# DeltaNet recurrence and low-rank mixer on one core: the engine order written by the program's own planner

## Chip, core and metric

One core of one Trainium2 chip. The metric is the device time of one execution, in microseconds. The engines are TensorE (PE; its weight loads are listed as PEld), VectorE (DVE), ScalarE (ACT), GpSimd (POOL) and SyncE (SP, which here only issues DMAs). Each runs its own instructions in order, and waits for the others through semaphores.

## What is computed

Four batches of eight heads, 768 positions, head size 48, go through a delta-rule recurrence. The result, seen as `x` of 4 x 768 x 384, goes through a mixer. q, k, v and beta are float32; U, V and the two channel weights arrive as float64.

```python
k_n = k / (norm(k, axis=-1) + 1e-6)
for t in range(768):                       # state: 48 x 48 per batch and head
    y[:, :, t] = q_t @ state
    state = state + beta_t * outer(k_t, v_t - k_t @ state)
x = y as (4, 768, 384)                     # heads side by side
u = x + transpose(transpose(x) @ U @ V)    # U: 768 x 32, V: 32 x 768
out = u + relu(u @ w_ch1) @ w_ch2          # w_ch1: 384 x 1536, w_ch2: 1536 x 384
```

## The kernel before

**Units.** A batch `b` is cut into 12 chunks of 64 positions. Six chunks are a unit, `n = 2b` and `n = 2b + 1`. Inside a chunk the recurrence becomes a triangular system, whose inverse is found per unit for all its chunks and heads at once; the chunks themselves then follow one another through the state. Each unit goes through these steps:

- `load(n)` (lines 199 to 212): 24 DMAs on SP, eight each for k, q and v. `kn` and `vn` have two buffers, `qn` has one.
- `norms(n)` (214 to 250): square, sum, root and reciprocal of the keys' length, and `vn` times the length on GpSimd (line 237); one small transpose and four DMAs give `cp`, the factors that the inversion needs.
- `grams(n)` (252 to 295): 24 transposes of k and q (line 264) and 96 products of k with k and q (line 276), copied to `pg` and `qk`.
- `blocks(n)` (297 to 350): `pg` goes through DRAM (four DMAs `scr`, line 303, one DMA `gs`, line 310) to 96 partitions of 32 x 32 blocks. 31 steps of two VectorE instructions (lines 324 and 330) invert them in `xt`. Another trip through DRAM (lines 336 to 349: one DMA out, six back) puts the result into `zt` and `zc`.
- `below(n)` (352 to 390): two rounds of 96 small matmuls (`p_x`, line 364, and `p_v`, line 379) fill the off-diagonal block of `zt`.
- `recur(b, c)` (398 to 488), per chunk: matmuls `p_b`, a subtraction on VectorE to `rhs`, `p_y`, then `p_c`, a copy on ScalarE to `z`, then `p_s`, an addition on VectorE to the state, and the second part of `p_y`, copied into `x`. Each chunk needs the state of the one before.

**Mixer.** `mixer(b)` (491 to 546) needs all 12 chunks of its batch. `p_tt` is the product with U (line 495). Then, for each half of 384 positions: three times `p_h` (product with V, line 507), its addition to `x`, and three transposes `p_u`, copied to `ut`; then 12 times `p_f` (line 521; three matmuls of 384 columns and a relu on ScalarE), and three times `p_o` (line 535; 12 matmuls, an addition, and the output DMA of line 545). A float32 matmul stands in the trace as two records, so the 72 program matmuls of `p_f` and `p_o` of one half are 144 records, and all eight halves are 1,152.

**Weights.** `load_weights` (148 to 194) turns 27 slices of float64 into float32, 15 of them w_ch1, V and U, 12 w_ch2. Each slice is one DMA on SP into `wide` (two buffers), seven integer and float instructions on VectorE and a last addition on GpSimd (line 192).

**Order.** Every step is a Python generator. A heap (lines 549 to 582) holds for each generator a due time that is written by hand, and emits the steps by due time: `FIRST, PERIOD = 95.0, 140.0`, one batch per period. The emitted order is what the framework's own scheduler starts from; it may still reorder instructions.

Of the kernel before, what the change touches and what calls it, by code (L numbers as in the profile page):

```python
# [25 lines left out]
def kernel(  # L26
# [64 lines left out]

    ident = const.tile([128, 128], FP32, name="ident")
# [20 lines left out]

    betas = const.tile([128, NC, 4 * B], FP32, name="betas")
# [5 lines left out]
    def load_beta():  # L120
        beta_sb = unit.tile([4 * B, NC, 2, L], FP32, name="beta_sb", tag="kq")
        for b in range(B):
            for g in range(2):
                nc.sync.dma_start(
                    out=beta_sb[4 * b : 4 * b + 4, :, g],
                    in_=beta[b, 4 * g : 4 * g + 4, :].rearrange("s (c t) -> s c t", t=L),
                )
        p_bt = ps_one([128, NC, 4 * B], "p_bt")
        for c in range(NC):
            nc.tensor.transpose(  # L130
                p_bt[:, c], beta_sb[:, c].rearrange("r g t -> r (g t)"), ident[0 : 4 * B, 0 : 4 * B]
            )
        nc.vector.tensor_copy(out=betas, in_=p_bt)

    WIDE = 384

    def weight_slices():
        for t in range(KT):
# [3 lines left out]
        for s0 in range(0, S, WIDE):  # L142
            yield v_sb[:, s0 : s0 + WIDE], moe_V[:, s0 : s0 + WIDE], None
        yield u_sb.rearrange("p c r -> p (c r)"), moe_U, NB
# [3 lines left out]
    def load_weights():  # L148
# [3 lines left out]

        for dst, src, groups in weight_slices():
# [4 lines left out]
            if groups:  # L158
                to = to.rearrange("p (c r) -> p c r", c=groups)
                src = src.rearrange("(c p) r -> p c r", c=groups)  # L160
            nc.sync.dma_start(out=to, in_=src)
            yield
# [5 lines left out]
                out=power, in0=h, scalar1=0x7FF00000, scalar2=None, op0=ALU.bitwise_and  # L168
            )
            nc.vector.tensor_scalar(  # L170
                out=power, in0=power, scalar1=float(896 << 20), scalar2=float(1151 << 20),
                op0=ALU.max, op1=ALU.min,
            )
            nc.vector.tensor_scalar(
                out=power, in0=power, scalar1=float(896 << 20), scalar2=8.0,
                op0=ALU.subtract, op1=ALU.mult,
            )
            nc.vector.scalar_tensor_tensor(
# [3 lines left out]
            nc.vector.tensor_scalar(  # L182
                out=upper, in0=h, scalar1=3, scalar2=0x007FFFFF,
                op0=ALU.logical_shift_left, op1=ALU.bitwise_and,
            )
            nc.vector.tensor_tensor(out=upper, in0=upper, in1=power, op=ALU.bitwise_or)
            rest = power.bitcast(FP32)
            nc.vector.scalar_tensor_tensor(  # L188
                out=rest, in0=low, scalar=2.0 ** -52, in1=rest,
                op0=ALU.mult, op1=ALU.mult,  # L190
            )
            nc.gpsimd.tensor_tensor(  # L192
                out=dst, in0=upper.bitcast(FP32), in1=rest, op=ALU.add
            )
# [4 lines left out]
    def load(n):  # L199

        b, hf = divmod(n, 2)
        vn = unit.tile([128, UC, 4, D], FP32, name="vn")
        for t, src in ((kns[n % 2], k), (qn, q), (vn, v)):
            for g in range(2):
                for s in range(4):
                    nc.sync.dma_start(
# [5 lines left out]
        raw[n] = vn  # L212

    def norms(n):

        b, hf = divmod(n, 2)
        kn, vn = kns[n % 2][:, :, :, 0:D], raw[n]
        ksq = single.tile([128, UC, 4, D], FP32, name="ksq", tag="gs")
# [5 lines left out]
        yield  # L224
# [12 lines left out]
        nc.gpsimd.tensor_tensor(  # L237
            out=vn, in0=vn, in1=norm[:, :, :, None].to_broadcast([128, UC, 4, D]), op=ALU.mult
        )
        yield  # L240
# [9 lines left out]
        made[n, "c"] = cp  # L250

    def grams(n):

        kn = kns[n % 2]
        kq = unit.tile([128, UC, 2, 2, 2 * L], FP32, name="kq")
# [41 lines left out]
    def blocks(n):  # L297
# [23 lines left out]
        for j in range(BK - 1):  # L321
# [11 lines left out]
            if j % 4 == 3:  # L333
                yield
# [278 lines left out]
```

## Time and profile before

| | us |
|---|---|
| median of three runs | 915.73 (910.38 to 916.62) |
| the profiled execution | 915.65 |
| its span, from the first to the last instruction | 913.9 |
| TensorE busy | 706.4 (77%) |
| VectorE busy | 362.9 (40%) |
| ScalarE busy | 178.6 (20%) |
| GpSimd busy | 59.3 (6%) |
[...]
| share of the 16 DMA engines taken by SP's queue | 20.8% |

TensorE has 7,484 matmul records, 1,152 of them the wide ones of the mixer. The page sums busy time over the span; matmuls overlap, so the sums of single lines are larger than their share of the engine. All DMAs of the program stand on one queue, SP's, 43.08 MB in 150,672 packets, most of them under 512 bytes.

### The profile page before, as it was taken

Reading aid. Unit: us, or ns where it says so; the run is one execution under the profiler, and the core shown is the slowest. Engines: PE = TensorE matmul, PEld = TensorE weight load, DVE = VectorE, ACT = ScalarE, POOL = GpSimd, SP = SyncE. Lnnn points to the kernel's source line nnn. Section 1 sums busy time; section 2 is a strip of 40 time slices with the busy share of each in tenths; the row PEclk is TensorE's granted clock in tenths of the full one; section 3 lists DMA queues with packets and bytes.
Section 4 is the critical chain, followed back from the end, with each engine's and each line's share of the span. In section 5 each row is a group of like instructions: output and inputs, shape, how many; then the busy total and the mean of one; then the engine's idle time right before and its main releaser. Section 6 shows DMA issues by size and latency. Waiting matters only on the chain.

```text
span 913.9 us, 17342 instructions
## 1 busy us (share of the span) xinstructions
PE 706.4 (77%) x7484; PEld 437.0 (48%) x7484; DVE 362.9 (40%) x930; ACT 178.6 (20%) x386; POOL 59.3 (6%) x66
## 2 busy tenths in 40 slices
PE   2305604778988998704899899947999999999898
PEld 1204503564554565504465465625655565455454
DVE  1595798455944611282237113561363110100000
ACT  2103100231222212301331034102420231020020
POOL 2102112110210000100000001000100000000000
PEclk9756555576998999855599799975899799989799
DMA  3534314343231201402230212122102000000000
GB/s 77 119 89 111 80 44 122 71 96 88 69 68 46 44 19 37 81 8 48 50 62 19 51 30 55 42 60 54 28 10 69 2 3 10 17 1 9 17 0 27
DMA packets 150748, 44.19 MB, mean 48 GB/s; under 512 B 142928, under 2 KB 146000, under 8 KB 150672
## 3 DMA queue, kind: packets, MB, share of 16 engines
q1 hardware_dynamic: 150672, 43.08, 20.8%
q8 instruction: 59, 0.97, 0.4%
q14 instruction: 17, 0.14, 0.0%
HBM read 31.95 MB, written 11.01 MB: 47 GB/s over the span
## 4 chain that ended last, share of the span: by engine, by line
PE 64%; DVE 22%; ACT 4%; DMA 3%; SPq 3%; issue 3%; POOL 1%; ACTq 0%; DVEq 0%
PE p_f L521 21%; PE p_o L535 18%; DVE xt L330 6%; DVE prod L324 5%; PE p_c L441 3%; PE p_h L507 3%; PE p_y L473 3%; PE p_t L264 2%; PE p_g L276 2%; PE p_s L455 2%; PE p_tt L495 2%; PE p_u L514 2%; PE p_y L429 2%; PE p_v L379 2%; PE p_x L364 2%
## 5 line engine op out<-in xcount | busy, mean ns | idle before, releaser
L521 PE MATMUL p_f<-ut,w_sb 128*128 128x384 f32 x576 | 223.2, 533 | 3.4 <-ACT ut L515 3.4
L535 PE MATMUL p_o<-w_sb,h_f 128*128 128x384 f32 x576 | 196.2, 494 | 1.8 <-POOL w_sb L192 1.8
L521 PEld LDWEIGHTS p_f<-ut,w_sb 128*128 128x128 f32 x576 | 111.6, 205 | 74.6 <-issue 14.9
L535 PEld LDWEIGHTS p_o<-w_sb,h_f 128*128 128x128 f32 x576 | 107.9, 191 | 72.9 <-POOL w_sb L192 2.0
L330 DVE TENSOR_TENSOR xt<-xt,prod 96x31 f32<-96x31 f32 (+15 forms) x248 | 89.5, 361 | 7.0
L324 DVE TENSOR_TENSOR prod<-gs,xt 96x31 f32<-96x31 f32 (+15 forms) x248 | 84.9, 342 | 7.3
L544 DVE TENSOR_TENSOR x<-x,p_o 128x384 f32<-128x384 f32 x24 | 13.3, 553 | 179.5 <-PE p_o L535 179.5
L529 ACT ACTIVATE h_f<-p_f 128x384 f32<-128x384 f32 x96 | 47.1, 490 | 134.2 <-PE p_f L521 133.8
L364 PE MATMUL p_x<-zt,pg 32*32 32x32 f32 x768 | 19.4, 211 | 44.4 <-DMA zt<-scr 44.4
L425 DVE TENSOR_TENSOR rhs<-vn,p_b 128x192 f32<-128x192 f32 x44 | 15.5, 353 | 92.5 <-PE p_b L417 92.5
L495 PE MATMUL p_tt<-x,u_sb 128*32 128x384 f32 x48 | 23.3, 610 | 31.6 <-POOL u_sb L192 28.6
L464 DVE TENSOR_TENSOR s<-s,p_s 128x192 f32<-128x192 f32 x40 | 14.1, 354 | 82.7 <-PE p_s L455 82.7
L364 PEld LDWEIGHTS p_x<-zt,pg 32*32 32x32 f32 x768 | 17.5, 126 | 53.2 <-issue 49.2
L264 PE MATMUL p_t<-ident,kn 128*128 128x128 f32 x96 | 30.8, 342 | 15.7 <-DMA kn<-in_k_dram 15.7
L482 ACT COPY x<-p_y 64x192 f32<-64x192 f32 x96 | 30.0, 313 | 52.1 <-PE p_y L473 51.5
L276 PE MATMUL p_g<-kq 48*64 48x128 f32 x768 | 35.6, 319 | 5.4 <-ACT kq L269 4.0
L441 PE MATMUL p_c<-rhs,zt 64*64 64x48 f32 x704 | 34.3, 246 | 6.8 <-DVE rhs L425 6.8
L515 ACT COPY ut<-p_u 128x384 f32<-128x384 f32 x24 | 11.5, 478 | 141.8 <-PE p_u L514 141.8
L441 PEld LDWEIGHTS p_c<-rhs,zt 64*64 64x64 f32 x704 | 29.5, 160 | 19.6 <-DVE rhs L425 18.0
L473 PE MATMUL p_y<-z,qk 64*64 64x48 f32 x768 | 36.6, 242 | 1.9 <-ACT z L449 1.9
L372 ACT COPY xz<-p_x 64x768 f32<-64x768 f32 x8 | 6.3, 792 | 150.3 <-PE p_x L364 150.3
L192 POOL TENSOR_TENSOR w_sb<-upper,power 128x384 f32<-128x384 f32 x24 | 24.7, 1028 | 158.9 <-DVE power L188 158.9
(69 smaller groups left out, 647.3 us busy)
## 6 DMA issues: line engine op xcount, KB each, us to landing
wide<-in_moe_w_ch_dram SPq DMA_DIRECT2D x24, 384.0 KB
kn<-in_k_dram SPq DMA_DIRECT2D x64, 72.0 KB
qn<-in_q_dram SPq DMA_DIRECT2D x64, 72.0 KB
vn<-in_v_dram SPq DMA_DIRECT2D x64, 72.0 KB
out_dram<-x SPq DMA_DIRECT2D x24, 192.0 KB
scr<-pg SPq DMA_DIRECT2D x32, 96.0 KB
gs<-scr SPq DMA_DIRECT2D x8, 384.0 KB
scr<-xt SPq DMA_DIRECT2D x8, 384.0 KB
```

The source lines that it names most:

```text
L264: nc.tensor.transpose(p_t[:, j, i], t[:, c, 2 * j : 2 * j + 2].rearrange("p s d -> p (s d)"), ident,)
L276: nc.tensor.matmul(p_g[cols, par, c, :, j], kq[rows, c0 + c, j, 0, cols], kq[rows, c0 + c, j, :, cols], start=True, stop=True,)
L324: nc.vector.tensor_tensor(out=prod, in0=gs[:, j : j + 1, j + 1 :].to_broadcast([NP, m, w]), in1=xt[:, 0:m, j : j + 1].to_broadcast([NP, m, ...
L330: nc.vector.tensor_tensor(out=xt[:, 0:m, j + 1 :], in0=xt[:, 0:m, j + 1 :], in1=prod, op=ALU.subtract)
L364: nc.tensor.matmul(p_x[BK * g : BK * g + BK, r, BK * (e % (2 * UC)) : BK * (e % (2 * UC)) + BK], pg[rows, r, c, j, 0:BK], zt[rows, r, c, j ...
L441: nc.tensor.matmul(p_c[half(g), 2 * j + par], zt[half(g), par, cu, j], rhs[half(g), 2 * j + par], start=True, stop=True,)
L473: nc.tensor.matmul(p_y[half(g), par, D * j : D * j + D], qk[half(g), par, cu, j], z[half(g), 2 * j + par], start=(c == 0 and j == 0), stop ...
L482: nc.scalar.copy(xs[b][half(c % 2), c // 2, 4 * D * g : 4 * D * (g + 1)].rearrange("p (j r d) -> p r j d", r=2, d=D), pair_of(p_y)[half(g)],)
L495: nc.tensor.matmul(p_t, u_sb[:, c], x[:, c], start=(c == 0), stop=(c == NB - 1))
L521: nc.tensor.matmul(p_f, w1_sb[:, t, f * 128 : (f + 1) * 128], ut[:, t], start=(t == 0), stop=(t == KT - 1),)
L529: nc.scalar.activation(h_f, p_f, ACTF.Relu)
L535: nc.tensor.matmul(p_o, hs[f][:, c * 128 - g : (c + 1) * 128 - g], w2_sb[:, f], start=(f == 0), stop=(f == FT - 1),)
```

## The change

The heap of due times goes. Each step now yields, ahead of its instructions, either keys to wait for or three estimates: its TensorE time, its VectorE time, and a delay until its follower is ready. `run` keeps one clock for TensorE and one for VectorE and always emits the part whose step can start first by these estimates; between equals the part that stands earlier in the list wins. The list has the fronts of the mixer first, then batch by batch the recurrence, loads, norms, grams and blocks, with the weights behind those of batch 0, and at the end the wide parts of the mixer. All of it is traced in `tc.manual_schedule()`: each engine's order is then the emitted one.

Estimates that matter below: a load is ready 8.0 us after it is emitted, `gs` 6.0 us after the grams, `zt` 6.0 us after the inversion. A load's 24 issues take no time in the estimate, nor does a weight slice's DMA.

Besides the order: (1) beta comes in two DMAs instead of eight, on ACT's queue, and half of the k and q loads of unit 0 go there too; (2) the weight slices are loaded from GpSimd's queue, and U and V come first; (3) a slice takes five VectorE instructions and one on ScalarE, none on GpSimd; (4) `vn` is scaled on VectorE; (5) the mixer is split into `front(b, i)` and `wide(b, i)`, and the front takes its PSUM from the buffers `one`, not `mix`; (6) unit 1 has buffers of its own for the inversion (those of `ut`), and may start its trip through DRAM while unit 0 is inverted; (7) `below` is a part of `blocks`; `recur` runs through a whole batch.

```diff
+    def run(parts):
+        waits = {}
+        ready = {}
...
+        while waits:
+            best = None
+            for i in sorted(waits):
+                step = waits[i]
+                while i in waits and isinstance(waits[i][0], tuple):
+                    keys = [k for k in waits[i] if k[1] >= 0]
+                    if not all(k in done for k in keys):
+                        break
+                    advance(i, max([ready[i]] + [done[k] for k in keys]))
...
+                pe, dve, _ = waits[i]
+                start = max(ready[i], clock["pe"] if pe else 0, clock["dve"] if dve and not pe else 0)
+                if best is None or start < best[0] - 1e-6:
+                    best = start, i
...
+            if pe:
+                clock["pe"] = end
+            if dve:
+                end = clock["dve"] = max(end, clock["dve"]) + dve
+            clock["now"] = end
+            advance(i, end + after)
...
-            nc.sync.dma_start(out=to, in_=src)
-            yield
+            nc.gpsimd.dma_start(out=to, in_=src)
+            return dst, wide
...
+            yield 0, 1.3, 0.8
...
             nc.vector.tensor_scalar(
-                out=power, in0=h, scalar1=0x7FF00000, scalar2=None, op0=ALU.bitwise_and
+                out=power, in0=h, scalar1=20, scalar2=0x7FF,
+                op0=ALU.logical_shift_right, op1=ALU.bitwise_and,
+            )
+            nc.scalar.activation(
+                power, power, ACTF.Relu, bias=bias_e[0:rows], scale=2.0 ** 23
             )
...
     def load(n):
         b, hf = divmod(n, 2)
+        yield ("grams", n - 1), ("rec", n - 2)
+        yield 0, 0, 0
...
+                    queue = nc.scalar if n == 0 and g == 1 and t is not vn else nc.sync
+                    queue.dma_start(
...
+        emitted(("load", n), 8.0)
...
-        nc.gpsimd.tensor_tensor(
+        nc.vector.tensor_tensor(
             out=vn, in0=vn, in1=norm[:, :, :, None].to_broadcast([128, UC, 4, D]), op=ALU.mult
         )
...
     def blocks(n):
+        pool, tag = (mix, "ut") if n == 1 else (single, None)
+        yield ("grams", n), ("inverted", n - 1 - (n == 1))
+        yield 0, 0, 6.0
...
+            yield 0, 2 * (m * w + 150) / 960, 0.0
...
+        emitted(("inverted", n), 0.0)
+        yield ("below", n - 1),
+        yield 0, 0, 6.0
...
+    def recur(b):
+        yield ("mixed", b - 2), ("rec", 2 * b - 1)
...
+            yield (1.1, 0.4, 0.2) if c > 0 else (0, 0, 0)
...
+            yield 0.6, 0, 0.9
...
+            yield 1.1, 0.4, 0.2
...
+    def front(b, i):
+        yield (
+            ("rec", 2 * b + 1), ("front", b - (i == 0), 1 - i), ("wide", b - 1, i), ("weights", FT + 1)
+        )
...
+    def wide(b, i):
+        yield ("front", b, i), ("narrow", b - (i == 0), 1 - i)
+        for f in range(FT):
+            yield 1.95, 0, 0
...
+    parts = [beta_thread()]
     for b in range(B):
+        parts += [front(b, 0), front(b, 1)]
+    for b in range(B):
+        parts.append(recur(b))
+        for n in (2 * b, 2 * b + 1):
+            parts += [load(n), norms(n), grams(n)]
+        parts += [blocks(2 * b), blocks(2 * b + 1)]
+        if b == 0:
+            parts.append(load_weights())
+    for b in range(B):
+        parts += [wide(b, 0), wide(b, 1)]
+    with tc.manual_schedule():
+        run(parts)
```

## Rows read from the trace of the kernel before

**Rows 1.** The page, part 2: TensorE's busy tenths in 40 slices.

```profile
PE   2305604778988998704899899947999999999898
```

**Rows 2.** Stretches: us; PE, PEld, DVE, ACT, POOL busy; clock, DMA share, GB/s.

```profile
40.00:60.00 20.00, 2.24 (x19) 1.22 (x19) 18.49 (x53) 0.58 (x1) 0.00 (x0) 0.50 0.39 91
...
0.00:217.80 217.80, 96.75 (x1699) 72.59 (x1699) 133.35 (x345) 40.24 (x83) 37.49 (x46) 0.62 0.40 92
...
217.80:913.90 696.10, 609.67 (x5786) 364.46 (x5786) 229.53 (x585) 138.40 (x303) 21.78 (x20) 0.88 0.15 35
...
700.00:720.00 20.00, 17.48 (x77) 8.69 (x77) 3.09 (x5) 1.93 (x4) 0.00 (x0) 0.74 0.19 41
```

**Rows 3.** SP's queue, first 40 us: start us, us of issuing, line, count.

```profile
6.43 5.38 SPq L206 DMA_DIRECT2D kn<-in_k_dram  x8
...
25.88 0.51 SPq L161 DMA_DIRECT2D wide<-in_moe_w_ch_dram  x1
...
30.10 2.14 SPq L303 DMA_DIRECT2D scr<-pg  x4
...
32.29 1.27 SPq L206 DMA_DIRECT2D kn<-in_k_dram  x2
```

**Rows 4.** Timeline of VectorE and TensorE, first 226 us: start us, us, line.

```profile
30.78 0.35 DVE L167 TENSOR_SCALAR power<-wide 128x384 int32<-128x384 int32 x1
...
37.51 1.22 DVE L312 TENSOR_TENSOR gs<-gs,cp 96x1024 f32<-96x1024 f32 x1 [3.67 <-DMA gs<-scr]
...
91.38 1.08 PE L441 MATMUL p_c<-vn,zt 64*64 64x48 f32 x14 [0.36 <-ACT zt L385]
...
203.69 1.09 PE L473 MATMUL p_y<-z,qk 64*64 64x48 f32 x16 [0.47 <-ACT z L449]
...
217.78 7.78 PE L521 MATMUL p_f<-ut,w_sb 128*128 128x384 f32 x18 [0.57 <-ACT ut L515]
```

**Rows 5.** Chain of waits that ended last: start us, us, what.

```profile
11.18 2.38 DMA kn<-in_k_dram
...
80.80 2.95 DMA zt<-scr
...
389.80 1.23 DVE gs L312
...
414.26 2.99 DMA scr<-xt
...
422.20 2.78 PE p_x L364 x94
...
887.15 23.23 PE p_o L535 x72
```

**Rows 6.** Timeline of TensorE at the full clock, later stretches.

```profile
377.99 1.16 PE L276 MATMUL p_g<-kq 48*64 48x128 f32 x32 [0.24 <-ACT kq L269]
...
719.36 1.79 PE L364 MATMUL p_x<-zt,pg 32*32 32x32 f32 x94
...
740.80 0.45 PE L455 MATMUL p_s<-z,kn 64*64 64x48 f32 x16
...
745.37 0.45 PE L455 MATMUL p_s<-z,kn 64*64 64x48 f32 x16
...
790.25 4.06 PE L495 MATMUL p_tt<-x,u_sb 128*32 128x384 f32 x12
...
803.45 1.01 PE L521 MATMUL p_f<-ut,w_sb 128*128 128x384 f32 x1 [0.57 <-ACT ut L515]
```

**Rows 7.** Groups by line and shape: count, busy us, mean ns, idle before.

```profile
L167 DVE TENSOR_SCALAR power<-wide 128x384 int32<-128x384 int32 x24 | 8.4, 350 | 5.4 <-POOL w_sb L192 4.7 <-POOL u_sb L192 0.7
...
L178 DVE SCALAR_TENSOR_TENSOR power<-wide,power 128x384 int32<-128x384 int32 x24 | 13.2, 551 | 0.3
...
L192 POOL TENSOR_TENSOR w_sb<-upper,power 128x384 f32<-128x384 f32 x24 | 24.7, 1028 | 158.9 <-DVE power L188 158.9
```

**Rows 8.** Line 227 alone: ns minimum, median, maximum; first, last start.

```profile
L227 DVE TENSOR_TENSOR rec<-rec x8: 171/977/1922, 18.3 to 645.1; 128x24 f32<-128x24 f32 x8
```

More of the change, by code (lines that the diff above doesn't have):

```diff
@@ L89, in ps_mix, with emitted, advance @@
         return psum.tile(shape, FP32, name=name, tag="mix", bufs=2)
+    done, clock = {}, {"now": 0.0, "pe": 0.0, "dve": 0.0}
+    def emitted(key, after=0.0):
+        done[key] = clock["now"] + after
+    def run(parts):
+        waits = {}
+        ready = {}
+        def advance(i, at):
+            try:
+                waits[i], ready[i] = next(parts[i]), at
+            except StopIteration:
+                waits.pop(i, None)
+        for i in range(len(parts)):
+            advance(i, 0.0)
+        while waits:
[7 more added lines that the diff above has]
+                    advance(i, max([ready[i]] + [done[k] for k in keys]))
+                if i not in waits or isinstance(waits[i][0], tuple):
+                    continue
+                pe, dve, _ = waits[i]
+                start = max(ready[i], clock["pe"] if pe else 0, clock["dve"] if dve and not pe else 0)
+                if best is None or start < best[0] - 1e-6:
+                    best = start, i
+            start, i = best
+            pe, dve, after = waits[i]
+            end = start + pe
+            if pe:
[4 more added lines that the diff above has]
+            advance(i, end + after)
     ident = const.tile([128, 128], FP32, name="ident")
@@ L160, in load_weights @@
                 src = src.rearrange("(c p) r -> p c r", c=groups)
-            nc.sync.dma_start(out=to, in_=src)
-            yield
+            nc.gpsimd.dma_start(out=to, in_=src)
+            return dst, wide
+        slices = list(weight_slices())
+        yield 0, 0, 0
+        loaded = [start(*slices[0])]
+        for i in range(len(slices)):
+            dst, wide = loaded.pop()
+            rows, n = dst.shape
+            if i + 1 < len(slices):
+                loaded.append(start(*slices[i + 1]))
+            yield 0, 1.3, 0.8
             h, low = wide[0:rows, :, 1], wide[0:rows, :, 0].bitcast(U32)
@@ L181, in load_weights @@
             )
[L182 to L187, printed above, removed]
             nc.vector.scalar_tensor_tensor(
-                out=rest, in0=low, scalar=2.0 ** -52, in1=rest,
+                out=dst, in0=mant, scalar=2.0 ** -20, in1=power.bitcast(FP32),
                 op0=ALU.mult, op1=ALU.mult,
             )
-            nc.gpsimd.tensor_tensor(
-                out=dst, in0=upper.bitcast(FP32), in1=rest, op=ALU.add
-            )
+            emitted(("weights", len(slices) - i))
     raw, made, xs, states = {}, {}, {}, {}
@@ L236, in norms @@
         )
[L237 to L240, printed above, removed]
+        yield 0.3, 1.3, 0.5
         p_ct = ps_one([CS, 128], "p_ct")
@@ L389, in below @@
             )
-        yield
+        emitted(("below", n), 2.0)
     def by_slot(t):
@@ L549 @@
-    heap = []
-    def at(time, dt, fn, *args):
-        heap.append((time, len(heap), dt, fn, args, None))
-    MIX_STEPS = 1 + (S // GT) * (4 * (GT // 128) + FT + 2 * (GT // 128))
-    FIRST, PERIOD = 95.0, 140.0
-    load_beta()
-    for n in range(2 * B):
-        b, hf = divmod(n, 2)
-        t0 = (-40.0, -18.0, 27.0, 50.0)[n] if n < 4 else FIRST + PERIOD * (b - 2) + 65.0 * (hf + 1)
-        at(t0, 0, load, n)
-        at(t0 + 3, 1, norms, n)
-        at(t0 + 4, 1, grams, n)
-        at(t0 + 14, 2.5, blocks, n)
-        at(t0 + 38, 1, below, n)
```

372 lines of the change are left out of this document (192 added, 180 removed).

## Prediction

> **What bounds the kernel now.** I read the slices of the page first, then the busy time by stretch, then the timeline of the start, and last the chain of waits. In the slices [rows 1] TensorE is at 0 to 6 tenths in the first seven and falls to 0 and 4 again in slices 18 and 19 and to 4 in slice 27; the reader is to see two stages, and holes in the second. The first wide matmul of the mixer, `p_f`, starts at 217.78 us [rows 4]. Until there TensorE is busy for 97 of 218 us at a mean clock of 0.62, VectorE for 133 [rows 2]. Then come 696.1 us with TensorE busy for 609.7 at a clock of 0.88. So stage one is a chain of latencies that runs through VectorE and DMAs; stage two is bound by TensorE, with 86 us of idle time and a clock that is not always the full one.
>
> **How much of stage two is work.** I price TensorE's work after 217.78 at the full clock [rows 6]:
> - wide matmuls: 23.23 us for 72 records [rows 5], 0.3226 each; 1,152 make 371.7.
> - a chunk of the recurrence: two `p_s` are 4.57 us apart with three pairs of wide records between them, 4.57 - 6 x 0.3226 = 2.63; 36 chunks of batches 1 to 3 make 95.
> - grams: three times 1.16 for `p_g`; a transpose of 128 columns at a third of `p_tt`'s 4.06 / 12 is 0.11, 24 of them 2.7; together 6.2, and five units (3 to 7; unit 2 is done by then) make 31.
> - `below`: `p_x` 1.79, `p_v` alike, 3.5; six units make 21.
> - fronts: 4.06 for `p_tt`, and six times 0.68 + 3 x 0.11, 10.1 per batch; less the first half of batch 0, which lies before, 34.
>
> Together 553 of 696. The lost 143 are 86 idle and some 57 of low clock (among the idle is the tail from the last `p_o`, 887.15 + 23.23, to the span's 913.9: 3.5).
>
> **Stage one, part by part.** *Start.* Beta's eight issues stand ahead of k's at 6.43 [rows 3]; they go to ACT's queue, with half of unit 0's k and q. An issue on SP takes 5.38 / 8 = 0.67 us, and the last lands 2.38 later [rows 3, 5]. Unit 0's keys could land at about 9.5 instead of 13.6. But the planner counts no DMA time for weights and puts two to three slices of conversion ahead of `norms(0)` on VectorE; I let POOL's queue begin at 6, an assumption, as it clears the program's buffers first, and the first slice land at 10. So I give back half: `grams(0)` ends at 27 instead of 30. On ACT's queue ten issues, 6.7 us, stand ahead of the first square, which needs the keys anyway.
>
> *SP's order, against the change.* Before, the heap's times put `blocks(0)` ahead of `load(1)`, yet `kn` issues stand between `scr` and `gs` [rows 3]: the framework filled SP's waits. Now the order is the program's, and `load(1)`, which waits for the same key and stands earlier in the list, is emitted ahead of `blocks(0)`: 24 x 0.67 = 16 us. SP, with `cp(0)` at 20 to 23 by estimate, issues the load until 39. From the first `scr` (30.10) to the product on `gs` (37.51) it is 7.4 us [rows 3, 4], so inversion 0 begins at 47 instead of 37.5.
>
> *Inversions.* Alone, one takes 414.26 - 389.80 - 1.23 = 23.2 us [rows 5]. Inversion 0 with its product and unit 1's norms and masks (6.7 by the planner's estimates, taken as 6) ends at 77. The way back through DRAM is 422.20 - 414.26 = 8.0 us [rows 5], and 7.6 lie between the last `zt` (83.75) and `p_c` (91.38) [rows 4, 5]: recurrence 0 begins at 93, where it began at 91. Then the gain: inversion 1 follows at once, since unit 1 has buffers of its own and the weights come after both in the list. Before, batch 0's twelve chunks took from 91.4 to 204.8 [rows 4], 113 us where twelve at 4.6 are 55; the rest was inversion 1, with weight slices between its steps. It ends now at 77 + 24.4 + 5 (the chunks' own VectorE steps, 12 x 0.4) = 107, recurrence 1 can begin at 123, and recurrence 0 (six chunks at 4.6, the spacing of rows 6) ends at 121. So batch 0 is through at 123 + 28 = 151 instead of 204.8 [rows 4].
>
> *Weights.* A slice takes 2 x 0.35 + 3 x 0.551 = 2.35 us of VectorE, not 3.05 [rows 7]; ScalarE's new instruction lies on an engine busy for 40 of 218 us [rows 2]. Some seven slices fit before inversion 0 and eight more between 107 and 151, the 15 that the front asks for. This is cover, not gain, as long as the slices land. A load on POOL's queue is not in this trace. On SP the first slice was issued at 25.88 and used at 30.78 [rows 3, 4], so at most 4.9 us; from above I bound it in rival C. I take 5: two in flight then cost (5 + 2.35) / 2 = 3.7 us a slice, a little over the planner's 3.4, so VectorE waits a few us in all. On POOL the clearing of `xt` (lines 316 and 317) is queued behind a slice's issue, which waits for a conversion two slices back; VectorE has that conversion ahead of the inversion too, so it costs nothing more. `vn` on VectorE costs about 1.4 us (1,152 against `gs`'s 1,024 elements in 1.22 us [rows 4]) times eight, and frees VectorE of GpSimd: the 24-element product of line 227 takes 0.17 at least and up to 1.92 [rows 8], I take it while GpSimd's product of line 237 runs. I put these at nothing together.
>
> *Front.* From the end of the recurrence to `p_f` it was 13.0 us [rows 4]; I add 4, since now all six pairs of `p_tt` (4.06 [rows 6]) come after it. `p_f` starts at 151 + 17 = 168.
>
> **Stage two.** The wide parts stand last in the list, so they fill whatever the others leave, and the fronts get other PSUM buffers and run under the previous batch's `p_o`. That removes two kinds of loss: TensorE waiting for an inversion (slices 18, 19 and 27 [rows 1]; one inversion stands from 389.80 to 422.20 [rows 5]), and fronts standing alone (790.25 to 803.45, 13.2 us for 7.1 of work [rows 6]). New waits come from estimates that are too short, because TensorE now has to stand at the place the planner chose:
> - load: 8.0 (plus 1.0 for the recurrence's end) against 16 issues at 0.67 and 2.38, 13.1. Four us for each of units 2 to 7, 24. Behind the waiting transposes stand the wide matmuls, and all follow.
> - the way back to `zt`: 6.0 against 8.0, six times 2, 12.
> - `gs`: 6.0 against 7.4, on VectorE, where `rhs` and `s` of the running recurrence are queued behind it, six times 1.4, 8.
>
> Together 44. A wait costs clock as well: the stretch from 700 has 2.5 us of idle time in a front and a clock of 0.74, that is 5.2 us lost to the low level [rows 2]. I add 28 for the six loads and six `zt`. S = 72, half of what is lost now. Its bounds: 20 (waits fall together, the clock holds) and 143 (nothing is won).
>
> **Sum.** 168 + 553 + 72 + 3.5 for the tail = 796.5, and 1.75 that the execution lies over its span: 798. The profiled execution (915.65) is at the median of the runs (915.73), so the sum can be set against that.
>
> **Rivals.**
> A. The waits hide: S near 20, and the start as computed: 168 + 553 + 20 + 5 = 746. For it: a late load and a late `zt` may fall in one stall; recurrence, inversion and wide work are independent. Against: 20 us with a clock of 0.74 from 2.5 us of idle.
> B. TensorE stands as much as before: S = 143, 168 + 553 + 143 + 5 = 869. SP's in-order queue is what would do it, a 16 us load ahead of an inversion's `zt`; it is emitted first whenever a recurrence ends just before an inversion.
> C. Slower: slices on POOL's queue starve. GpSimd's addition took 1.03 us [rows 7]; if issuing a slice took as long, and only VectorE's idle time counted (1.51 of 20 us from 40 to 60 [rows 2]), a slice would come every 13.6 us. All 27 gate `p_o`: 6 + 27 x 13.6 = 373 instead of 168 + 23 = 191; some 50 us of recurrence and grams can be done meanwhile, so 798 + 182 - 50 = 930. It decides from about 13 us a slice. For it: rows 8. Against: what was waited out there is at most 1.75 us, and a conversion's instructions are 0.35 to 0.55 long [rows 7].
> D. The order comes out no better than the framework's: waits move from inversions to loads in both stages, about 915.
>
> [...]
>
> **Chances and range.** The forecast's case (750 to 845) 0.58, A 0.20, B 0.13, C 0.05, D 0.04. A measurement of this kernel can tell about 1% from no change. Faster by over 1% is the forecast, A and B: 0.91; within 1% D: 0.04; slower C: 0.05. The range goes down to `p_f` at 150 with S = 20 (728, rounded to 725) and up to `p_f` at 190 with S = 130 (878, rounded to 880); C, D and the ends of A and B stay out, under 2 in 10.
>
> **What would show it.** Right: `p_f` first at about 168; TensorE busy in nearly all of every slice from there, with short idle times put down to `kn` or `qn` (four us) and to `zt`; SP's queue with 24 issues between `cp(0)` and the first `scr`; no front standing alone. Wrong: VectorE waiting for `wide` (then C), idle times of 10 us at `p_x` with a load in front on SP (then B), a clock near 1.0 through stage two (then A), or `p_f` as late as 200.

## The result and the profile after

The changed kernel takes 854.9 us (median; 850.8 to 858.9), the kernel before 915.6 (910.4 to 916.6). The ratio is 0.934, with a 95% interval of 0.929 to 0.939. So the change gains 61 us where 118 were forecast; the time lies 57 us over the predicted one and inside the range. The profiled execution took 850.8 us, its span is 849.1.

Page of the kernel after, part 2: TensorE's busy tenths, and the granted clock in tenths of the full one, in 40 slices.

```profile
PE   3430567758995899887989898998988999999998
...
PEclk9765555675997999986999999998989899999999
```

Against [rows 1] the deep holes of stage two are gone. One is left, slice 13 (255 to 276 us, 5 tenths); behind it no slice is under 7. The start is still half idle, 112 of 211 us busy.

Stretches of the kernel after (columns as in [rows 2]): to the first matmul of recurrence 0, to recurrence 1, to its end, to the first `p_f`, and stage two.

```profile
0.00:98.00 98.00, 30.89 (x484) 24.18 (x484) 61.61 (x157) 20.65 (x36) 12.26 (x28) 0.70 0.45 88
98.00:137.10 39.10, 27.63 (x670) 24.74 (x670) 19.21 (x54) 9.20 (x23) 1.61 (x3) 0.50 0.30 62
137.10:178.30 41.20, 29.66 (x554) 25.20 (x555) 20.12 (x48) 14.63 (x33) 3.00 (x6) 0.58 0.45 95
178.30:211.00 32.70, 23.86 (x113) 11.89 (x114) 16.04 (x35) 9.00 (x17) 3.52 (x5) 0.60 0.48 107
211.00:849.10 638.10, 580.42 (x5702) 350.28 (x5700) 226.04 (x593) 136.75 (x304) 10.20 (x18) 0.94 0.18 40
```

Stage two fell from 696.1 us, with 86 idle, to 638.1, with 57.7 idle and a clock of 0.94 instead of 0.88. Against the sum, 553 + 72 + 3.5 = 628.5, it is 10 too long. Stage one is 211 instead of 168, 43 too long. Of the 57 us, then, most lie in stage one; some 4 are between the profiled execution and the median.

SP's queue at the start of the kernel after (columns as in [rows 3]).

```profile
25.53 5.40 SPq L266 DMA_DIRECT2D kn<-in_k_dram  x8
31.04 5.30 SPq L266 DMA_DIRECT2D qn<-in_q_dram  x8
36.38 5.36 SPq L266 DMA_DIRECT2D vn<-in_v_dram  x8
41.83 2.40 SPq L381 DMA_DIRECT2D scr<-pg  x4
...
179.80 5.43 SPq L266 DMA_DIRECT2D kn<-in_k_dram  x8
185.28 6.00 SPq L266 DMA_DIRECT2D qn<-in_q_dram  x8
191.37 6.37 SPq L266 DMA_DIRECT2D vn<-in_v_dram  x8
```

The 24 issues of `load(1)` stand ahead of the first `scr`, as forecast. The rows from 179.80 on are `load(3)`; the next rows show what it does there.

Timeline of VectorE and TensorE of the kernel after: start us, us, line, in brackets the idle time before and what ended it.

```profile
49.61 1.22 DVE L392 TENSOR_TENSOR gs<-gs,cp 96x1024 f32<-96x1024 f32 x1 [10.54 <-DMA gs<-scr]
...
137.14 1.09 PE L524 MATMUL p_c<-rhs,zt 64*64 64x48 f32 x16 [1.41 <-DVE rhs L508]
...
149.48 1.35 DVE L291 TENSOR_REDUCE norm<-kq 128x24 f32<-128x1152 f32 x1 [7.21 <-ACT kq L289]
...
178.19 5.91 PE L585 MATMUL p_tt<-x,u_sb 128*32 128x384 f32 x12
185.89 0.30 PE L338 MATMUL p_t<-ident,kn 128*128 128x128 f32 x1 [1.79 <-DMA kn<-in_k_dram]
193.03 0.48 PE L338 MATMUL p_t<-ident,qn 128*128 128x128 f32 x1 [6.84 <-DMA qn<-in_q_dram]
...
211.02 2.92 PE L623 MATMUL p_f<-ut,w_sb 128*128 128x384 f32 x6
```

Between `p_tt` and `p_f` the front of batch 0 is not alone. Transposes of unit 3 stand in TensorE's order between its matmuls and wait, 1.79 and 6.84 us, for a load that SP began to issue only at 179.80; the rest of those transposes and most of unit 3's products follow between the front's matmuls. The front, 17 us by the forecast, takes 33. The same holds for unit 2 in recurrence 1: VectorE stands 7.21 us at unit 2's norm, with the recurrence's own steps behind it, and recurrence 1 takes 41 us instead of 28.

### The profile page after: what moved, and what is told of

The parts are those of the page before. It is cut to its first block, busy times and chain, and to the rows that moved or that the text cites. A ratio compares the mean times of both kernels' runs of the same rounds, so it can differ in the third digit from the quotient of the medians.

```text
span 849.1 us, 17340 instructions
## 1 busy us (share of the span) xinstructions
PE 692.5 (82%) x7520; PEld 436.3 (51%) x7520; DVE 343.0 (40%) x884; ACT 190.2 (22%) x413; POOL 30.6 (4%) x59
## 4 chain that ended last, share of the span: by engine, by line
PE 55%; DVE 17%; DMA 11%; SPq 8%; ACT 4%; issue 3%; POOL 1%; DVEq 0%; ACTq 0%; POOLq 0%
PE p_o L640 17%; PE p_f L623 17%; DVE xt L411 6%; DVE prod L405 5%; SPq L266 4%; PE p_c L524 3%; PE p_g L350 3%; DMA scr<-xt 3%; PE p_h L597 2%; PE p_y L554 2%; DMA gs<-scr 2%; PE p_t L338 2%; DMA scr<-pg 2%; PE p_s L538 2%; SPq L424 2%
## 5 line engine op out<-in xcount | busy, mean ns | idle before, releaser
L640 PE MATMUL p_o<-w_sb,h_f 128*128 128x384 f32 x576 | 209.2, 510 | 1.5 <-DVE w_sb L247 1.5
L623 PE MATMUL p_f<-ut,w_sb 128*128 128x384 f32 x576 | 208.1, 508 | 0.0
L623 PEld LDWEIGHTS p_f<-ut,w_sb 128*128 128x128 f32 x576 | 108.0, 196 | 69.9 <-issue 8.7
L411 DVE TENSOR_TENSOR xt<-xt,prod 96x31 f32<-96x31 f32 (+15 forms) x248 | 83.9, 338 | 8.7 <-DVE prod L405 0.3
L444 PE MATMUL p_x<-zt,pg 32*32 32x32 f32 x768 | 20.3, 216 | 49.9 <-DMA zt<-scr 49.7
L338 PE MATMUL p_t<-ident,qn 128*128 128x128 f32 x96 | 31.3, 341 | 23.9 <-DMA qn<-in_q_dram 18.8
L350 PEld LDWEIGHTS p_g<-kq 48*64 48x64 f32 x768 | 27.1, 166 | 31.3 <-ACT kq L343 21.7
L524 PEld LDWEIGHTS p_c<-rhs,zt 64*64 64x64 f32 x704 | 29.0, 158 | 18.3 <-issue 11.3
L343 ACT COPY kq<-p_t 128x512 f32<-128x512 f32 x48 | 27.9, 584 | 37.0 <-PE p_t L338 34.7
L532 ACT COPY z<-p_c 128x192 f32<-128x192 f32 x48 | 15.3, 319 | 91.5 <-PE p_c L524 91.2
```

What stands on the lines that cost most here:

```text
L338: nc.tensor.transpose(p_t[:, j, i], t[:, c, 2 * j : 2 * j + 2].rearrange("p s d -> p (s d)"), ident,)
L350: nc.tensor.matmul(p_g[cols, par, c, :, j], kq[rows, c0 + c, j, 0, cols], kq[rows, c0 + c, j, :, cols], start=True, stop=True,)
L411: nc.vector.tensor_tensor(out=xt[:, 0:m, j + 1 :], in0=xt[:, 0:m, j + 1 :], in1=prod, op=ALU.subtract)
L444: nc.tensor.matmul(p_x[BK * g : BK * g + BK, r, BK * (e % (2 * UC)) : BK * (e % (2 * UC)) + BK], pg[rows, r, c, j, 0:BK], zt[rows, r, c, j ...
L524: nc.tensor.matmul(p_c[half(g), 2 * j + par], zt[half(g), par, cu, j], rhs[half(g), 2 * j + par], start=True, stop=True,)
L623: nc.tensor.matmul(p_f, w1_sb[:, t, f * 128 : (f + 1) * 128], ut[:, t], start=(t == 0), stop=(t == KT - 1),)
```

## The experiments

Each edit is against the kernel after, but for the eighth. For all of them, the median time, the ratio to the kernel before, the first `p_f`, and stage two with TensorE's idle time in it. The last three columns are of the profiled execution, which can lie some us off the median (836.3 in e10):

| run | us | ratio (95%) | `p_f` | stage two | idle in it |
|---|---|---|---|---|---|
| kernel after | 854.9 | 0.934 (0.929, 0.939) | 211.0 | 638.1 | 57.7 |
| e1_honest | 832.4 | 0.909 (0.908, 0.911) | 187.8 | 643.3 | 48.0 |
| e2_qpool | 851.3 | 0.930 (0.927, 0.932) | 205.8 | 644.7 | 57.0 |
| e3_scrfirst | 851.7 | 0.931 (0.927, 0.936) | 212.8 | 635.0 | 59.1 |
| e4_weights_sp | 868.9 | 0.949 (0.947, 0.951) | 232.3 | 637.0 | 58.2 |
| e5_no_manual | 823.5 | 0.898 (0.892, 0.905) | 225.3 | 592.8 | 20.6 |
| e6_late23 | 860.1 | 0.938 (0.935, 0.942) | 177.5 | 679.3 | 69.9 |
| e7_honest_scr | 831.9 | 0.908 (0.904, 0.911) | 188.1 | 642.9 | 48.3 |
| e8_parts_old_order | 907.4 | 0.990 (0.986, 0.994) | 216.8 | 688.4 | 82.4 |
| e9_honest_free | 807.0 | 0.881 (0.878, 0.885) | 212.8 | 595.3 | 17.7 |
| e10_manual_pe | 843.4 | 0.922 (0.916, 0.928) | 221.4 | 613.3 | 46.8 |
| e11_free_pe | 838.2 | 0.917 (0.914, 0.920) | 212.1 | 621.3 | 39.9 |
| e12_hand_start | 782.3 | 0.856 (0.854, 0.859) | 186.4 | 593.4 | 16.8 |

How much work lies in stage two differs a little with where units 2 and 3 fall: TensorE has 5,702 records there in the kernel after and 5,701 in e5, 5,785 in e1, e9 and e12, 5,906 in e6. The 84 between the first two groups are 20 transposes and 64 products of unit 3, 4.5 us by the prices of the prediction. So stage two is compared between runs of like counts: after with e5, e1 with e12.

**Longer estimates (e1_honest).** Theory 1: work stands in the order ahead of its data because the estimates are too short. In the diff they are those of a load, of `gs` and of `zt`.

```diff
-        emitted(("load", n), 8.0)
+        emitted(("load", n), 14.0)
...
-        yield 0, 0, 6.0
+        yield 0, 0, 8.0
...
-        yield 0, 0, 6.0
+        yield 0, 0, 8.5
```

> The changed kernel with three estimates brought to the measured lengths: a load is ready after 14.0 instead of 8.0 us, gs after 8.0 instead of 6.0, zt after 8.5 instead of 6.0. Nothing else. Theory 1 (the first wide matmul comes late, at 211 instead of 168 us, because TensorE's order puts the transposes of units 2 and 3 ahead of their data, and everything behind them waits): the waits for qn at 141 to 147 and 184 to 193 us go, p_f starts at about 195, and stage two loses its waits for zt too; the time falls by 15 to 30 us, to 825 to 840. Theory 2 (it is the sharing of TensorE, PSUM, ScalarE and VectorE between the running recurrence and the next unit, not the late data): p_f within 5 us of 211, the time within 1%.

832.4 us. Recurrence 1 (from its first `p_c`), the front and stage two of this run:

```profile
137.69:170.54 32.85, 25.70 (x562) 22.18 (x557) 17.98 (x44) 14.87 (x34) 2.68 (x5) 0.65 0.45 105
170.54:187.80 17.26, 12.78 (x34) 4.62 (x31) 11.46 (x25) 4.16 (x9) 2.15 (x4) 0.70 0.84 183
187.80:831.10 643.30, 595.31 (x5785) 360.94 (x5784) 226.60 (x593) 140.23 (x310) 9.79 (x17) 0.92 0.18 40
```

Recurrence 1 takes 33 us and the front 17.3, against 28 and 17 in the forecast: unit 3 is no longer in the front, while unit 2's 24 transposes and 96 products are still in recurrence 1. Three constants bring 22 us, and all of it in stage one; they were changed together, so this run doesn't part them. In stage two the waits of `p_x` for `zt` fall from 18.3 to 3.3 us, as theory 1 had it, but the stretch is no shorter: it has the 84 records more, and a clock of 0.92 for 0.94.

**q on another queue (e2_qpool).** Is it the time of issuing on SP that makes the loads late?

```diff
-                    queue = nc.scalar if n == 0 and g == 1 and t is not vn else nc.sync
+                    queue = nc.scalar if n == 0 and g == 1 and t is not vn else nc.gpsimd if n > 0 and t is qn else nc.sync
```

> The changed kernel with the q loads of units 1 to 7 issued on GpSimd's queue instead of SP's, so that k and q are issued side by side: 8 issues, 5.4 us, and 2.4 to land make 7.8, what the planner assumes. Estimates stay. Theory 1 (late data at a fixed place in TensorE's order): like the run with the longer estimates, p_f at about 195 and 15 to 25 us less in all; scr of unit 0 also moves up by 5 us, since eight issues less stand ahead of it. Theory 2 (sharing): p_f within 5 us of 211. Third possibility: on POOL the q loads stand behind weight slices that wait for conversions, so q comes no earlier for units 1 to 3, and only units 4 to 7 gain, some 5 us.

851.3 us, not to be told from the kernel after.

```profile
175.19 5.44 SPq L266 DMA_DIRECT2D kn<-in_k_dram  x8
...
184.21 0.30 PE L338 MATMUL p_t<-ident,kn 128*128 128x128 f32 x1 [3.85 <-DMA kn<-in_k_dram]
...
189.25 1.64 PE L597 MATMUL p_h<-tt,v_sb 32*128 32x384 f32 x2 [3.21 <-DVE tt L590]
```

In these rows, SP's queue and TensorE in the front, unit 3's transposes still stand between the front's matmuls; they now wait for `kn`. Over stage one the waits of `p_t` for `qn` fell from 15.6 to 5.5 us, and `p_f` came 5 us earlier, which stage two gave back. The third possibility falls: q of units 2 and 3 is issued at 124.94 and 173.72, 11 us ahead of the kernel after. But `kn` of unit 3, still on SP, is issued only at 175.19, and TensorE stands 3.85 us for it. This speaks for the place in the order more than for the queue.

**The first trip through DRAM ahead of the load (e3_scrfirst).** This undoes what the prediction called SP's order, against the change.

```diff
-        yield ("grams", n - 1), ("rec", n - 2)
+        yield ("grams", n - 1), ("rec", n - 2), ("scr", 0 if n == 1 else -1)
...
         nc.sync.dma_start(out=gs, in_=scr)
+        emitted(("scr", n))
```

> The changed kernel with load(1) emitted behind the DRAM trip of blocks(0) on SP, as the framework's order had it before; all else the same. If SP's order at the start is on the path, gs of unit 0 is multiplied at about 38 instead of 49.6 us, and inversion 0, recurrence 0 and p_f come 8 to 12 us earlier; the time falls by 8 to 12. If the start is bound elsewhere (unit 1's data now come 3 to 6 us later, and inversion 1 follows), p_f stays within 4 us of 211.

851.7 us, no gain. VectorE's timeline, then SP's, of this run:

```profile
43.49 1.22 DVE L393 TENSOR_TENSOR gs<-gs,cp 96x1024 f32<-96x1024 f32 x1 [3.08 <-DMA kn<-in_k_dram]
...
45.72 0.22 DVE L412 TENSOR_TENSOR xt<-xt,prod 96x60 f32<-96x60 f32 x1
54.13 1.35 DVE L291 TENSOR_REDUCE norm<-kq 128x24 f32<-128x1152 f32 x1 [8.19 <-ACT kq L289]
...
83.26 0.31 SPq L419 DMA_DIRECT2D scr<-xt  x1
```

The inversion begins six us earlier and stops after two steps. Unit 1's norm stands in VectorE's order inside it, and its load is now the late one: 8.19 us idle. The inversion ends at 83 instead of 81. The 16 us of SP's order were real and bought nothing when taken away, since they moved to the next thing in a fixed order.

**Weights back on SP (e4_weights_sp).**

```diff
-            nc.gpsimd.dma_start(out=to, in_=src)
+            nc.sync.dma_start(out=to, in_=src)
```

> The changed kernel with the weight slices issued on SP's queue again, as before, in the same planned order. If the separate queue is what keeps the planned order from blocking, each slice's issue, which waits for the conversion two slices back, now stands in front of loads and DRAM trips: 20 to 60 us slower. If the queue makes no difference (SP has time to spare), within 1%.

868.9 us, 14 more by the medians (20 by the profiled executions), and less than I expected. The first `scr` is issued at 49.41 instead of 41.83 and `p_f` comes 21 us later; stage two is the same. So the separate queue is worth that much at the start, and nothing later.

**No order by hand (e5_no_manual).** The planner emits as before, but the framework may move an instruction whose input is late behind others of its engine.

```diff
-    with tc.manual_schedule():
-        run(parts)
+    run(parts)
```

> The changed kernel without manual_schedule: the planner's emission is what the framework's scheduler starts from, and it may reorder each engine, as in the kernel before. Theory 1 (much of what is lost comes from instructions standing in front of data that is late, and the framework moves others ahead): SP's load of unit 1 is broken up by scr again, the transposes of unit 3 go behind the front, and the time falls to 830 to 845. Theory 2 (the planner's order is what gains, and the framework's own estimates undo it): slower, 870 to 910.

823.5 us, 31 less and below theory 1's range. Windows of this run:

```profile
0.00:225.26 225.26, 108.95 (x1821) 83.77 (x1821) 140.25 (x376) 59.45 (x118) 23.84 (x49) 0.62 0.44 96
225.26:818.10 592.84, 572.23 (x5701) 341.44 (x5700) 190.20 (x509) 132.99 (x295) 5.93 (x10) 0.96 0.18 38
```

With the same count of records, stage two is 45 us shorter: 37 less idle and 8 less busy, at a clock of 0.96 for 0.94. Stage one is 14 longer. VectorE runs 376 instructions in it instead of 292, weight slices that the free order pulls ahead of the inversions: the `gs` product of unit 0 starts at 63.83 instead of 49.61, right behind a slice. Neither of theory 1's two signs came: all of unit 1's load still stands ahead of the first `scr` (37.41), and unit 3's transposes still stand in the front. So the gain is of stage two alone.

**Loads 2 and 3 held until the front is out (e6_late23).**

```diff
-        yield ("grams", n - 1), ("rec", n - 2)
+        yield ("grams", n - 1), ("rec", n - 2), ("front", 0 if n in (2, 3) else -1, 0)
```

> The changed kernel with load(2) and load(3) held until front(0, 0) has been emitted; estimates as they were. This takes units 2 and 3 out of recurrence 1 and out of the front. If late data in front of the path's work costs the 30 us between 137 and 211, p_f starts at 175 to 185, since nothing of units 2 and 3 stands ahead of it; but their inversions start some 50 us later, so stage two has more waits for zt: the whole lies between 835 and 860. If the 30 us are the recurrence's and the front's own (low clock, the conversions between them), p_f stays above 200.

860.1 us. Recurrence 1 and the front of this run:

```profile
138.38:162.43 24.05, 19.43 (x433) 17.57 (x433) 15.88 (x40) 8.75 (x22) 3.22 (x6) 0.50 0.65 150
162.43:177.46 15.03, 12.27 (x32) 4.38 (x30) 9.89 (x22) 4.53 (x9) 1.61 (x3) 0.73 0.36 106
```

`p_f` is at 177.5, recurrence 1 takes 24 and the front 15: units 2 and 3 were what made both long. But stage two takes 679.3, 41 more. Of these, 12 are idle time and some 11 the 204 more records at the prices of the prediction; the rest goes with a clock of 0.90 for 0.94. What is held back is done in stage two at a greater price: 34 us gained, 41 given back. So the length of the two stretches is the fault of units 2 and 3, but leaving them out is no cure.

**Longer estimates and the trip first (e7_honest_scr).** The edits of e1, with 8 kept for unit 0's load, and those of e3 (two places are shown).

```diff
-        emitted(("load", n), 8.0)
+        emitted(("load", n), 14.0 if n else 8.0)
...
         nc.sync.dma_start(out=gs, in_=scr)
+        emitted(("scr", n))
```

> The three longer estimates (load 14.0 for units 1 to 7, but 8.0 for unit 0, whose k and q are issued on two queues; gs 8.0; zt 8.5) together with load(1) behind the DRAM trip of blocks(0). With the short estimates that move gained nothing, since VectorE's order had unit 1's norms inside inversion 0 and waited there for unit 1's keys. If that is the reason, the move now pays: gs of unit 0 at about 41 us, inversion 0 ended by 74, p_f at 175 to 180 and 8 to 12 us less than with the estimates alone, 820 to 825. If the start is bound by something else, within 1% of 832.

831.9 us, the same as e1; the further gain I expected did not come. `scr<-xt` of unit 0 is at 80.46 instead of 85.48, and recurrence 1 begins at 133.63 instead of 137.69, yet `p_f` is at 188.1 against 187.8. This is recurrence 1 of this run; that of e1 is shown there:

```profile
133.63:172.31 38.68, 32.05 (x562) 27.56 (x557) 18.94 (x45) 15.05 (x34) 2.77 (x6) 0.50 0.43 92
```

The same 562 records take 5.8 us more at a granted clock of 0.50, the lower level throughout, where e1 has 0.65. So the move pays until recurrence 1 begins, and the four us are lost there to the clock, not to another late transfer as in e3. Why the clock rose within e1's recurrence and not within this one, the runs don't show.

**The parts without the order (e8_parts_old_order).** The kernel before, with its own emission and order, and in it the changed conversion, the changed queues of beta, of unit 0's k and q and of the weights, and `vn` on VectorE (the core of the edit):

```diff
-            nc.sync.dma_start(out=to, in_=src)
+            nc.gpsimd.dma_start(out=to, in_=src)
...
-        nc.gpsimd.tensor_tensor(
+        nc.vector.tensor_tensor(
             out=vn, in0=vn, in1=norm[:, :, :, None].to_broadcast([128, UC, 4, D]), op=ALU.mult
         )
```

> The kernel before, with its heap of due times and the framework's order, but with the parts of the change that are not order: five-plus-one conversion, weight slices on GpSimd's queue, vn on VectorE, beta in two DMAs and half of unit 0's loads on ACT's queue. If the planned order carries the gain, 900 to 915. If the shorter conversion and the queues carry it, below 880.

907.4 us: 9 of the 61 us. The rest needs the new order (that of the weight slices with it, U and V first, which this run doesn't have), the separate fronts or unit 1's own buffers; this run doesn't part these.

**Both levers (e9_honest_free).** The edits of e1 (one of the three is shown) and of e5.

```diff
-        emitted(("load", n), 8.0)
+        emitted(("load", n), 14.0)
...
-    with tc.manual_schedule():
-        run(parts)
+    run(parts)
```

> Longer estimates (load 14, gs 8, zt 8.5) and no manual order: the emission is the planner's, the framework may move an instruction whose input is late behind others on its engine. Both levers act on the same loss, work that stands in an engine's order ahead of its data. Theory 1 (each repairs its own part: the estimates the start, where the first wide matmul fell from 211 to 188 and recurrence 1 to front from 33 to 17 us; the free order stage two, which fell from 638 to 593): 188 + 593 = 781 plus 2 around it, at best; with the start of the run without manual order, 225, less 10 to 20, plus 593: 800 to 810. I take 800, range 780 to 815. Theory 2 (the framework's reordering makes the planner's estimates idle, since it looks at readiness by its own reckoning): the same as with the free order alone, 823 plus or minus 6. Theory 3 (the manual order is needed at the start, and longer estimates hold work back that the framework would have filled in): 830 or more.

807.0 us, in theory 1's range though over its 800: the two add up (22 + 31 = 53 of 855 would give 802). Stage two is 595.3 with 17.7 idle, with 84 records more than e5; the start is 12.5 us shorter than e5's, though still 25 longer than e1's.

**Which engine's fixed order (e10_manual_pe, e11_free_pe).** The hand order on TensorE alone, then on all engines but TensorE.

```diff
-    with tc.manual_schedule():
+    with tc.manual_schedule(engines={mybir.EngineType.PE}):
```

> The kernel after with the hand order kept on TensorE alone; SyncE, VectorE, ScalarE and GpSimd may be reordered by the framework. It tells which engine's fixed order costs the 31 us between 854.9 (all fixed) and 823.5 (all free). Theory 1 (the loss is TensorE's own in-order queue: transposes of a late unit and p_x ahead of ready wide matmuls): nothing is regained, 845 to 858. Theory 2 (the loss is the queue of loads on SyncE, where gs and zt issues stand behind 24 load issues, and VectorE's order): most of the 31 us comes back with the TensorE order untouched, 820 to 835; SyncE's list shows the scr issues ahead of part of the loads again. Half and half: 836 to 844.

```diff
-    with tc.manual_schedule():
+    with tc.manual_schedule(engines={mybir.EngineType.SP, mybir.EngineType.DVE, mybir.EngineType.Activation, mybir.EngineType.Pool}):
```

> The mirror of it: TensorE may be reordered, the other four engines keep the order of the program. Theory 1 (TensorE's in-order queue is the loss): 820 to 835, and the wait of p_x for zt (50 us over the span, 18 of them in stage two) shrinks under 25 us. Theory 2 (SyncE's and VectorE's order is the loss): 845 to 858, the waits stay where they are, p_x for zt above 40. If the framework's order of TensorE suits the fixed orders of the others badly, it is slower than 858.

843.4 and 838.2 us: of the 31 us, freeing the other four engines brings 11.5 and freeing TensorE 16.7. e10 is in the half-and-half case of its expectation, e11 a little over theory 1's range. Neither queue is the culprit alone. By the table both gain in stage two, 25 and 17 us, and e10 loses 10 at the start. In e11 the wait of `p_x` for `zt` in stage two, 18.3 us in the kernel after, is down to 3.6 (over the span from 49.7 to 34.1, where theory 1 asked for less than 25), with the program's order kept on SP; so part of that wait was TensorE's place in the order, not a late transfer.

**Order by hand for the start only (e12_hand_start).** With e1's estimates.

```diff
             advance(i, end + after)
+            if ("front", 0, 0) in done:
+                hand.close()
...
-    with tc.manual_schedule():
-        run(parts)
+    hand = ExitStack()
+    hand.enter_context(tc.manual_schedule())
+    run(parts)
+    hand.close()
```

> The longer estimates (load 14, gs 8, zt 8.5); the hand order holds on every engine until the first half of the mixer's front has been emitted, and the framework may reorder all that comes behind. The start's lists are those of the run with longer estimates and the hand order, stage two is left free. Theory 1 (the loss is separable: the start wants the planner's order with honest estimates, stage two wants an order that can yield to late data): first wide matmul at 188 as in that run, stage two 593 to 600 as in the two free runs (593, 595), so 781 to 788 plus 2: 785, range 778 to 795. Theory 2 (a fixed order in stage one moves conversions and loads to where stage two needs them late, so stage two grows as the start shrinks, as it did when loads 2 and 3 were held back: minus 34, plus 41): first wide matmul 188, stage two 612 or more, 800 to 808, not distinguishable from the free order with the same estimates (807). Theory 3 (the free part pulls transposes and norms of units 2 and 3 ahead of the front): first wide matmul at 205 or later, 805 or more.

782.3 us (780.6 to 783.4), the best version here, 73 less than the kernel after. Windows of this run:

```profile
137.03:169.77 32.74, 25.54 (x561) 22.01 (x557) 17.86 (x44) 14.87 (x34) 2.68 (x5) 0.66 0.47 106
169.77:186.43 16.66, 12.62 (x35) 4.63 (x31) 11.77 (x26) 4.74 (x10) 2.14 (x4) 0.70 1.01 188
186.43:779.80 593.37, 576.56 (x5785) 345.45 (x5784) 224.32 (x592) 140.72 (x309) 8.89 (x16) 0.97 0.19 43
```

The start is e1's and stage two is e9's: theory 1, and the losses are separable. Against e1, with the same records in stage two, it is 50 us: 31 of idle time, and 19 of busy time at a clock of 0.97 instead of 0.92. The start wants the planner's order, with weights behind the inversions; the rest wants an order that gives way to late data. The same split with the short estimates was not run.

## Why the prediction was right in direction and short in size

Right: faster, and not by the single parts (e8: 9 us) but by the order and what goes with it. The step that failed is the walk through stage one, from inversion 1 to `p_f`.

- *Start.* The `gs` product of unit 0 came at 49.6 (47 forecast, 37.5 before) and recurrence 0 at 98.0 (93). SP's order was seen and priced about right. Undone, it brought no gain in the end (e3, e7).
- *Inversions.* Inversion 1 follows inversion 0 at once, as forecast. They end at 81.1 and 115.5 (77 and 107), and from the second to recurrence 1 it is 21.6 us (16), so recurrence 1 starts at 137 instead of 123. On that way `p_x` and `p_v` stand between chunks of recurrence 0 and take 2.76 and 2.77 us at a clock of 0.50, not the 1.79 of [rows 6] (at 0.93).
- *Recurrence 1*, 28 forecast, took 41, and the *front*, 17 forecast, took 33. This is the term that was mis-sized: 29 of the 43 us. I counted the chunks and the front alone, though the planner has units 2 and 3 in these stretches. With units 2 and 3 held back the two take 24 and 15 (e6), with longer estimates 33 and 17.3 (e1), here 41 and 33. So 24 of these 74 us go with the longer estimates, and 11 more with the work of the units itself. The clock has a share in both differences that these runs don't part: it is 0.58 and 0.60 here, 0.65 and 0.70 in e1, and e7 shows 5.8 us from it alone; `p_tt` takes 5.91 at a clock of 0.68 instead of 4.06 at 1.00 [rows 6]. Nor is it all TensorE's order: without the transposes `p_h` would still have waited for `tt`, which VectorE copies at 188.81, 4.7 us after `p_tt` ended, behind a weight slice and the first steps of inversion 2. I had one mechanism, late loads at the place that the planner chose, but charged it to stage two, at 24 us for units 2 to 7; the units' own work in these stretches I put at nothing.
- *Stage two.* S was 72, and with the tail's 3.5 the sum has 75.5 over the 553; the measured figure is 638.1 - 553 = 85. The idle time without the tail is 54 (44 forecast), and the rest, 580.4 - 553, is 27 (28 forecast). The 553 also count 4.5 us of unit 3 that lie before `p_f`. The sums agree within some 15 us, the parts do not, so their agreement is partly luck.

TensorE's waits in stage two of the kernel after: total us, times, longest.

```profile
PE p_x L444 <- DMA zt<-scr: 18.3, 11, 7.3
PE p_b L500 <- DVE s L551: 5.5, 3, 3.8
PE p_v L459 <- ACT xz L452: 3.8, 2, 2.0
PE p_s L538 <- DVE qk L363: 3.3, 3, 1.6
PE p_h L597 <- DVE tt L590: 3.2, 2, 2.2
PE p_t L338 <- DMA qn<-in_q_dram: 3.2, 4, 1.0
```

The loads cost 3.2 us where I put 24, the trips to `zt` 18.3 where I put 12, and the remainder is many short waits for VectorE and ScalarE that I had not priced. The later loads cost TensorE little because it came to them later than the plan counts: its first transposes of units 4 to 7 start 10.9 to 12.0 us after the load's first issue, and it waits at most 1.0 us for q. Those of unit 3 start after 6.1 us; those of unit 2 after 12.0, and there the long wait was VectorE's. These are SP's and TensorE's rows of unit 5:

```profile
381.34 5.48 SPq L266 DMA_DIRECT2D kn<-in_k_dram  x8
393.36 0.33 PE L338 MATMUL p_t<-ident,kn 128*128 128x128 f32 x1
```

Why TensorE came later there, the runs don't show. The longest wait for `zt` lies in the one hole left, slice 13:

```profile
254.73 7.58 PE L640 MATMUL p_o<-w_sb,h_f 128*128 128x384 f32 x23
269.60 0.31 PE L444 MATMUL p_x<-zt,pg 32*32 32x32 f32 x2 [7.29 <-DMA zt<-scr]
```

This is TensorE's timeline: wide work is at hand on both sides of `p_x`, and the fixed order makes it wait. The fronts no longer stand alone, as forecast (`p_h`'s waits for `tt` are 3.2 us in all).

- *Rival C* fell. First the page's part 6 of the kernel after (the last number is the median in us from issue to landing), then VectorE's waits:

```profile
wide<-in_moe_w_ch_dram POOLq DMA_DIRECT2D x24, 384.0 KB, 3.7
```

```profile
DVE power L226 <- DMA wide<-in_moe_U_dram: 10.9, 1, 10.9
```

A slice lands in 3.7 us in the median, 4.7 at most; I took 5. VectorE's one real wait for a slice is the first, at the very start, and the separate queue is worth 14 us (e4). A slice's issue on GpSimd takes 0.54 us in the median, not the 1.03 of rival C, and nothing of C's 13.6 us a slice is to be seen in these rows.
- *Rivals A, B and D.* S without the tail is 81.5, against the forecast's 72, A's 20 and B's 143. A free order comes nearest to A: 593.4 - 553 = 40 in e12. D fell with the result; e8 shows what the old order makes of the new parts, 907.

That e12 comes out near the forecast, 782 against 798, doesn't make the sum right: it has `p_f` at 186 instead of 168 and S at 37 instead of 72.

## What to carry to other kernels

A program's plan is only as good as its worst estimate where its order is binding: count a load's issues and its landing, and walk each stretch of the critical path with all that the plan puts there, next units' loads included. Fix the order by hand only for as long as a fixed order wins (here the start, where it keeps weights behind the inversions), and leave the rest to a scheduler that can pass late work by: with the longer estimates the same instructions took 832 us bound throughout, 807 free throughout, and 782 bound for the start alone. Moving one late transfer earlier in a fixed order moved the wait to its neighbour (e3).

## What the runs showed of the hardware that was not expected

A one-input instruction of VectorE took three to four times its usual length, 1.18 and 1.38 us, where GpSimd cleared a tile beside it. These are rows of VectorE's and GpSimd's timelines, kernel after, start us and us:

```profile
37.03 1.18 DVE L226 TENSOR_SCALAR power<-wide 128x384 int32<-128x384 int32 x1 [1.38 <-DMA wide<-in_moe_w_ch_dram]
...
37.05 0.95 POOL L396 MEMSET xt<- 96x1024 f32 x1
...
177.78 1.38 DVE L226 TENSOR_SCALAR power<-wide 128x384 int32<-128x384 int32 x1
...
177.98 0.97 POOL L396 MEMSET xt<- 96x1024 f32 x1
...
181.84 1.22 DVE L392 TENSOR_TENSOR gs<-gs,cp 96x1024 f32<-96x1024 f32 x1 [1.82 <-DMA cp<-cts]
...
181.90 1.26 POOL L397 COPY xt<-cp 96x32 f32<-96x32 f32 x1 [2.95 <-DMA cp<-cts]
```

The instruction, 0.364 us in the median of 27, took 1.18 and 1.38, and ended 0.2 us after the memset both times. The kernel before has such a case in line 167, 0.350 us in the median of 27: one on half the columns took 1.12 from 145.13 on, beside a memset of 0.95 from 145.18, and ended 0.12 after it. Single instructions are as long in e3 (1.06) and e5 (1.10), and one of line 233 in e6 (1.25); what GpSimd did beside those is not shown. One two-input product of the kernel before (line 227) kept its length, 0.17 us at 72.95, beside a memset from 72.56 to 73.50. Two of line 229, 0.184 us in the median of eight, began beside a memset and ran into GpSimd's addition behind it; they took 1.34 and 1.81 and ended 0.05 us after the addition.

The last pair of rows is the other way round: GpSimd's copy, 0.24 us at most in its other seven cases, took 1.26 beside VectorE's two-input product and ended 0.1 us after it. And line 227's product of 24 elements took 1.77 to 1.92 us in four of the eight cases of [rows 8], and ended 0.04 to 0.05 us after GpSimd's product of `vn` (line 237) each time; after that product had left GpSimd, it took 182 to 184 ns in all eight cases (line 299 there), as the prediction guessed. VectorE's row starts first in all three pairs above, by 0.02 to 0.2 us, and is the lengthened one in two of them, so the order of the starts doesn't tell which is lengthened. Why the two lengthen each other, the runs don't show.
